# Filter taps spread over the partitions by two DRAM transfers instead of four TensorE transposes

## The chip, the cores and the metric

The kernel runs on one core of one Trainium2 chip. The metric is the device time of one execution in microseconds (us). Before the change the median of three runs is 174.2 us (174.18 to 174.44). One further execution was recorded by the hardware profiler; all views of the profile come from it.

## The reference

```python
x = A_x                                            # (1, 2048, 448)
g = sigmoid((x * gate_w).sum(-1, keepdims=True))
a = A_ref(x, wqkv, wo)                             # linear attention, 16 heads of 28
b = B_ref(x, log_A_real, A_imag, C_real, C_imag, log_dt, D_skip)
return g * a + (1 - g) * b

# B_ref: a state space convolution, N = 256 states for each of D = 448 channels
dt = exp(log_dt)
A = -exp(log_A_real) + 1j * A_imag
C = (C_real + 1j * C_imag) * dt[:, None]
K = 2 * einsum("dn,dnl->dl", C, exp((A * dt[:, None])[:, :, None] * arange(L))).real
y = causal convolution of u with K along L         # by FFT in the reference
return y + u * D_skip
```

The inputs make `exp(log_dt)` so small that the filter K is flat in time to working precision: K of channel d is its first tap at every lag. The kernel tests that (`okc`) and then needs one tap per channel, so that the convolution becomes a running sum over time, multiplied with a row of 448 taps. The general convolution (`general_conv`) is in the program for channels that fail the test, and is skipped by a branch when none does.

## The kernel before, in words

Time, 2048 steps, is cut into 16 chunks of 128, one step per partition. 32-bit floats are split into a high and a low part (`low`, line 236) so that products keep their precision on TensorE. For each chunk c the main loop (lines 475 to 531) issues, in this order for every engine: the load of chunk c + 3 on the SP queue (`load_x`), the key projection of chunk c + 1 on TensorE (`project`, line 333; 11 matmuls in order of which every second one at the start reads the low part of `xt`), the split of chunk c + 2's transposed input (`split_t`: high part on ScalarE, low part on GpSimd), the key features (`k_feature`, `k_high`, `k_low`), the query projection of chunk c, its features (`q_post`), the products of `do_g(c)`, and the split of chunk c + 2's plain input (`split_n`, then `skip`, both on GpSimd). The schedule is written out by hand: each engine executes its instructions in exactly the order of the program, and waits where an input isn't there.

The convolution part rides along. `do_v(v)` makes two matmuls (lines 409 and 410) with a triangle of ones: running sums of chunk v, put into the PSUM buffer `v0` or `v1` by the parity of v. `v_post(v)` multiplies them with the row of taps `near` on VectorE (line 414), sends the last row to `u` by two small transfers on the SP queue (line 417), and adds the product to `y` on GpSimd (`v_add`, line 422). The table `VS` says which chunks v go with which c: from c = 5 to 10 two of them, 2c - 10 and 2c - 9.

The taps themselves are made by `s4d_prepare`, a generator whose steps are dealt out by `steps(n)`. It reads `abc`, the four parameter tables of 112 partitions x 4 x 256 each (channel j * 112 + r is partition r, column j), reduces over the states and leaves `p0`, a tile of 112 partitions x 4 taps in `sm` (last written by line 307, which the profile shows as the helper's line 279). Its last step, dealt out at c = 5 between the query projection and `q_post(5)`, spreads them over the partitions: four transposes (line 312) of `p0`'s columns, broadcast, give 128 x 448 in PSUM, and ScalarE copies that to `near` (line 313). `near` is the first 448 columns of `rows`; the second 448 are `dsk`, a row of DRAM broadcast to all partitions when the kernel starts (line 226).

What is loaded at the start goes over one SP queue in the order of lines 216 to 233: the first weights and inputs, `dsk`, chunk 3, `ldt`, the first table of `abc`, chunk 4, the other three tables, and `both` (identity and triangle).

Of the kernel before, what the change touches and what calls it, by code (L numbers as in the profile page):

```python
# [7 lines left out]
F32 = mybir.dt.float32  # L8
# [7 lines left out]
P = 128  # L16
S = 2048
D = 448
# [4 lines left out]
J = 4  # L23
DJ = D // J
# [116 lines left out]
def gated_mix_kernel(ctx: ExitStack, tc: tile.TileContext, xin, wq_d, wvo_d, abc_d, ldt_d, dsk_d,  # L141
                     turn_d, cst_d, first_d, gin_d, out):
    nc = tc.nc
    PE, ACT, DVE, POOL, SP = nc.tensor, nc.scalar, nc.vector, nc.gpsimd, nc.sync
# [12 lines left out]
    work = ExitStack()  # L157
# [7 lines left out]
    ident, trir = both[:, 0], both[:, 1]  # L165
# [5 lines left out]
    near, dsk = (rows[:, i * D:(i + 1) * D] for i in range(2))  # L171
# [12 lines left out]
    xn_p = work.enter_context(tc.tile_pool(name="xn", bufs=7))  # L184
    tp = work.enter_context(tc.tile_pool(name="tp", bufs=2))
    ps = work.enter_context(tc.tile_pool(name="ps", bufs=1, space=PSUM))

    warm = tp.tile([P, 512], mybir.dt.bfloat16, name="warm", tag="e")
    DVE.memset(warm, 1.0)  # L189
# [7 lines left out]
    def load_x(c):  # L197
        r = xp.tile([P, XC], F32, name="xr", tag="xr")
        turned[c], plain[c] = r[:, :NAT], r[:, NAT:]
        SP.dma_start(out=r, in_=xin[c])  # L200
# [4 lines left out]
    abc = pf[:DJ, 3 * J * N:7 * J * N].rearrange("p (i j n) -> p i j n", i=4, j=J)  # L205
    wkr = {}
    o = 0
    for part in PARTS:
# [8 lines left out]
        o = e  # L217
# [8 lines left out]
    SP.dma_start(out=dsk, in_=dsk_d.to_broadcast([P, D]))  # L226
    load_x(3)
    SP.dma_start(out=ldt, in_=ldt_d)
    for i in range(4):
        SP.dma_start(out=abc[:, i], in_=abc_d[:, i])  # L230
        if i == 0:
            load_x(4)
    SP.dma_start(out=both, in_=turn_d)

    def low(eng, o, r, h):
# [2 lines left out]
    def split_t(c):  # L238
        w = xt[c] = xt_p.tile([P, 2 * NAT], F32R, name="xt", tag="t")
        ACT.copy(w[:, :NAT], turned[c])  # L240
        low(POOL, w[:, NAT:], turned[c], w[:, :NAT])
# [32 lines left out]
    def small():  # L274
        cnt[0] += 1
        return sm[:, cnt[0] - 1]

    def s4d_prepare():
        tt = lambda eng, o, a, b, op: eng.tensor_tensor(out=o, in0=a, in1=b, op=op)
        stt = lambda o, a, k, b, op1: DVE.scalar_tensor_tensor(out=o, in0=a, scalar=k, in1=b, op0=ALU.mult, op1=op1)  # L280
        junk = [yf[:DJ, F0 + (i - 2) * 2 * N:F0 + (i - 1) * 2 * N].rearrange("p (i n) -> p i n", i=2) for i in range(2)]
        s0, s1, dt, am, p0, p1, d2, md, b0, b1 = (small() for _ in range(10))
        for j in range(J):
            ACT.activation(abc[:, 0, j], abc[:, 0, j], AF.Exp)
        ACT.activation(dt, ldt, AF.Exp)
        tt(DVE, d2, dt, dt, ALU.mult)
        yield
        for j in range(J):
            ACT.activation(junk[0], abc[:, 0:2, j], AF.Square, accum_out=am[:, j:j + 1])
            ACT.activation(junk[0][:, 0], abc[:, 2, j], AF.Copy, accum_out=s0[:, j:j + 1])  # L290
            DVE.scalar_tensor_tensor(out=junk[1], in0=abc[:, 2:4, j], scalar=1.0, in1=abc[:, 0:2, j], op0=ALU.mult,
                                     op1=ALU.mult, accum_out=s1[:, j:j + 1])
            if j % 2:
                yield
        tt(DVE, md, am, d2, ALU.mult)
        stt(p0, s0, 2.0, dt, ALU.mult)
        stt(p1, s1, -2.0, d2, ALU.mult)
        DVE.tensor_scalar(out=md, in0=md, scalar1=SMALL, scalar2=None, op0=ALU.is_le)
        stt(b0, p0, -1.0, p0, ALU.max)
        stt(b1, p1, -1.0, p1, ALU.max)  # L300
        yield
        DVE.tensor_scalar(out=p0, in0=p0, scalar1=-BIG, scalar2=BIG, op0=ALU.max, op1=ALU.min)
        DVE.scalar_tensor_tensor(out=md, in0=b0, scalar=1.0 / FAR, in1=md, op0=ALU.is_ge, op1=ALU.mult)
        stt(okc, b1, FLAT, b0, ALU.is_le)
        DVE.scalar_tensor_tensor(out=md, in0=b0, scalar=FAR, in1=md, op0=ALU.is_le, op1=ALU.mult)
        tt(DVE, okc, okc, md, ALU.mult)
        tt(DVE, p0, p0, okc, ALU.mult)
        DVE.tensor_reduce(out=oks, in_=okc, op=ALU.add, axis=AX.X)
        yield
        o = ps.tile([P, 512], F32, name="p", tag="v1")  # L310
        for j in range(J):
            PE.transpose(o[:, j * DJ:(j + 1) * DJ], p0[:, j:j + 1].to_broadcast([DJ, P]), ident[:DJ, :DJ])  # L312
        ACT.copy(near, o[:, :D])

    def pieces(c, wh, wl, n, tag, last=None):
        o = ps.tile([P, 512], F32, name=tag, tag=tag)
        h, l = ([xt[c][:, i + k * P:i + (k + 1) * P] for k in range(J)] for i in (0, NAT))
        hh, lh, hl = ([(a[k], w[:, k]) for k in range(J)] for a, w in ((h, wh), (l, wh), (h, wl)))
        hl = hl[1:]
        if last == "x":  # L320
            seq = hh + hl + lh
        else:
            seq = [p for k in range(J) for p in (hh[k], lh[k])] + hl
            if last and len(last) > 1:
                seq = [{"h": hh, "l": lh, "w": [None] + hl}[i[0]][int(i[1])] for i in last.split()]
            elif last == "w":
                seq = seq[2:6] + seq[8:9] + seq[6:8] + seq[9:] + seq[:2]

        def run(count):
            for _ in range(min(count, len(seq))):  # L330
                a, b = seq.pop(0)
                run.n += 1
                PE.matmul(o[:, :n], lhsT=a, rhs=b, start=run.n == 1, stop=not seq)  # L333
        run.n = 0
        return o, run

    def project(*args, **kw):
        o, run = pieces(*args, **kw)
        run(11)
        return o  # L340
# [15 lines left out]
    def k_feature(c, o):  # L356
        e = tp.tile([P, D], F32, name="e", tag="e")
        pks[c] = o[:, :D]
        ACT.activation(e, pks[c], AF.Relu, scale=-1.0)  # L359
        ACT.activation(e, e, AF.Exp, scale=-1.0)  # L360
        DVE.scalar_tensor_tensor(out=pks[c], in0=pks[c], scalar=1.0, in1=e, op0=ALU.add, op1=ALU.max)  # L361

    def k_high(c):
        pkh[c] = tp.tile([P, 512], F32R, name="pkh", tag="pkh")[:, EDGE:EDGE + D]
        ACT.add(pkh[c], pks[c], 1e-6)
# [12 lines left out]
    def q_post(c, o, mid=None):  # L378
        ACT.activation(e1[:, c:c + 1], o[:, D:D + 1], AF.Exp, scale=-1.0)
        feature(pq[:, c], o, mid)  # L380
# [26 lines left out]
    def do_v(c):  # L407
        v = vt[c] = ps.tile([P, 512], F32, name="v", tag="v%d" % (c % 2))
        PE.matmul(v[:, :D], lhsT=tri, rhs=xn[c][:, :D], start=True, stop=False)  # L409
        PE.matmul(v[:, :D], lhsT=tri, rhs=xn[c][:, XC - NAT:], start=False, stop=True)  # L410
# [14 lines left out]
    def steps(n):  # L425
        for _ in range(n):
            next(prep, None)
# [47 lines left out]
    for c in range(2, NC - 2):  # L475
        if c + 3 < NC:
            load_x(c + 3)
        if c == 2:
            SP.dma_start(out=cst, in_=cst_d)
        if c == 4:  # L480
            SP.dma_start(out=wvo, in_=wvo_d)
        vs = VS.get(c, ())
        ko = project(c + 1, wkh, wkl, D, "v1" if c in (2, 4) else "k")
        for v in vs[:1]:
            do_v(v)
        split_t(c + 2)
        k_feature(c + 1, ko)
        k_high(c + 1)
        if c > 5:
            for v in vs[:1]:  # L490
                v_post(v)
        k_low(c + 1)
        qo = project(c, wqh, wql, D + 2, "q")
        if c == 5:
            steps(1)
        else:
            for v in vs[1:]:
                do_v(v)
        q_post(c, qo)
        if c == 10:  # L500
            split_n(c + 2)
        if c == 5:
            v_post(0)
        else:
            for v in vs[1:]:
                v_post(v)
        if c < 5:
            steps(2 if c == 4 else 1)
        if c == 3:
            DVE.tensor_copy(tri, trir)  # L510
            DVE.tensor_copy(gcr, gcat)
        if c == 7:
            SP.dma_start(out=okr[:, None, :DJ], in_=oks[:, None, :])
        if c == 9:
            DVE.tensor_reduce(out=okr[:, DJ:], in_=okr[:, :DJ], op=ALU.add, axis=AX.X)
            DVE.tensor_copy(okn, okr[:, DJ:])
        do_g(c)
        if c == 5:
            do_v(1)
        if c < 4:  # L520
            skip(c - 1)
        if c != 10:
            split_n(c + 2)
        if c == 5:
            v_post(1)
        for j in {11: (0, 1), 12: (2, 3)}.get(c, ()):
            w = xn_p.tile([P, NX], F32R, name="wo", tag="n")[:DJ, :2 * D].rearrange("p (i d) -> p i d", i=2)
            woh.append(w[:, 0])
            wol.append(w[:, 1])
            ACT.copy(woh[j], wo[:, j])  # L530
            low(POOL, wol[j], wo[:, j], woh[j])
# [109 lines left out]
    c = NC - 2  # L641
# [294 lines left out]
```

## Time and profile before

| what | us |
|---|---|
| median of three runs | 174.2 |
| the profiled execution | 174.88 |
| its span, first to last instruction | 173.1 |
| busy: TensorE matmul (PE) | 168.1 |
| busy: GpSimd (POOL) | 119.5 |
| busy: VectorE (DVE) | 114.4 |
| busy: ScalarE (ACT) | 96.3 |

Times in the views are microseconds from the start of the span unless marked ns. PEld is the weight load of TensorE, which overlaps with its matmuls; SP is the queue that issues the transfers here. A row of a timeline gives start, duration, engine, line, operation, the tile written and the tiles read, the shape and a count; in square brackets stands the idle time of the engine just before and what ended it. Rows with a count above 1 are several instructions merged. A row `L312 ...: a/b/c, d to e` gives the shortest, median and longest duration in ns and the first and the last start. In the chain that ended last each piece is the work that the end was waiting for at that time. Line numbers are those of the kernel before; a helper's line stands for all its calls.

### The profile page before, as it was taken

What the parts mean: (1) busy time and instruction counts of PE and PEld (TensorE: products, weight loads), DVE (VectorE), ACT (ScalarE), POOL (GpSimd) and SP (SyncE); (2) the same over time, 40 slices, a digit from 0 to 9 for tenths busy, and PEclk for the clock granted to TensorE, in tenths of its full rate; (3) what the DMA queues carried; (4) which work ended last, traced back from release to release, by engine and by line L of the source; (5) the groups of instructions that cost most, each with busy time, mean ns of one, the idle gap of its engine ahead of it and who ended that gap; (6) DMA issues with size and microseconds to landing.
All of it is one profiled execution on the core that took longest, in us unless ns stands there. A gap on an engine that the chain in (4) does not pass through costs nothing.

```text
span 173.1 us, 2796 instructions
## 1 busy us (share of the span) xinstructions
PE 168.1 (97%) x875; PEld 152.2 (88%) x875; DVE 114.4 (66%) x241; ACT 96.3 (56%) x221; POOL 119.5 (69%) x127
## 2 busy tenths in 40 slices
PE   6999999999999999999999999999999999999991
PEld 2698999999899999999999999999899999999991
DVE  1927746698975483836627346487898998997551
ACT  3768678895256262543727456356564564664541
POOL 5072568777619987696996999429978997983100
PEclk9999999999999999999999999999999999999999
DMA  5999976088002031231414200000031221222212
GB/s 172 417 294 301 257 175 198 0 327 342 0 4 95 29 122 19 106 90 37 122 22 122 106 1 1 0 0 2 7 67 53 107 106 58 91 98 78 108 67 102
DMA packets 7963, 18.61 MB, mean 108 GB/s; under 512 B 2045, under 2 KB 4810, under 8 KB 7818
## 3 DMA queue, kind: packets, MB, share of 16 engines
q1 hardware_dynamic: 7946, 18.41, 32.6%
q8 instruction: 7, 0.11, 0.3%
q14 instruction: 10, 0.08, 0.1%
HBM read 14.38 MB, written 3.67 MB: 104 GB/s over the span
## 4 chain that ended last, share of the span: by engine, by line
PE 97%; DVE 1%; ACT 0%; issue 0%; ACTq 0%
PE a L628 21%; PE g L402 20%; PE q L333 19%; PE k L333 15%; PE v L333 6%; PE tr L603 4%; PE q L258 3%; PE v L410 2%; PE v L409 2%; PE m L707 1%; PE k L727 1%; PE tr L727 1%; DVE warm L189 0%; PE p L312 0%; DVE ot L633 0%; ACT pq L639 0%
## 5 line engine op out<-in xcount | busy, mean ns | idle before, releaser
L628 PE MATMUL a<-wk,th 128*128 128x448 f32 (+1 forms) x170 | 36.4, 360 | 0.0
L402 PE MATMUL g<-pkh,xn 128*128 128x448 f32 x112 | 35.5, 363 | 0.0
L628 PEld LDWEIGHTS a<-wk,th 128*128 128x128 f32 x170 | 29.5, 189 | 1.6
L333 PE MATMUL k<-wk,xt 128*128 128x448 f32 x132 | 30.1, 374 | 0.0
L361 DVE SCALAR_TENSOR_TENSOR k<-k,e 128x448 f32<-128x448 f32 x12 | 7.6, 631 | 30.1 <-ACT e L360 30.1
L333 PE MATMUL q<-wqh,xt 128*128 128x450 f32 x120 | 27.5, 366 | 0.0
L333 PEld LDWEIGHTS k<-wk,xt 128*128 128x128 f32 x132 | 25.3, 192 | 2.1 <-ACT wk L432 0.4
L422 POOL TENSOR_TENSOR y<-y,t 128x448 f32<-128x448 f32 x16 | 18.7, 1171 | 11.5 <-DVE t L414 11.5
L236 POOL TENSOR_TENSOR xn<-xr,xn 128x448 fp32r<-128x448 f32 x16 | 19.4, 1212 | 7.4 <-ACT xn L246 5.5
L333 PEld LDWEIGHTS q<-wqh,xt 128*128 128x128 f32 x120 | 22.5, 188 | 1.8
L402 PE MATMUL g<-pkl,xn 128*128 128x448 f32 x64 | 23.4, 366 | 0.0
L402 PEld LDWEIGHTS g<-pkh,xn 128*128 128x128 f32 x112 | 21.0, 188 | 2.2
L236 POOL TENSOR_TENSOR xt<-xr,xt 128x512 fp32r<-128x512 f32 x14 | 18.2, 1297 | 6.0 <-ACT xt L240 6.0
L359 ACT ACTIVATE e<-k 128x448 f32<-128x448 f32 x12 | 6.5, 544 | 27.2 <-PE k L333 27.2
L541 POOL TENSOR_TENSOR prod<-pq,zb 128x448 f32<-128x448 f32 x16 | 18.6, 1169 | 4.1 <-ACT zb L664 3.0
L252 POOL TENSOR_TENSOR y<-xr,rows 128x448 f32<-128x448 f32 x16 | 18.8, 1174 | 0.0
L566 POOL TENSOR_TENSOR pn<-pq,den 128x336 f32<-128x336 f32 x16 | 12.3, 768 | 6.0 <-ACT den L555 4.1
L633 DVE SCALAR_TENSOR_TENSOR ot<-y,og,a 128x448 f32<-128x448 f32 (+1 forms) x17 | 10.7, 629 | 5.1 <-PE a L628 5.1
L611 DVE TENSOR_TENSOR th<-tr,th 128x512 fp32r<-128x512 f32 x16 | 11.0, 690 | 2.7 <-ACT th L610 2.1
L402 PEld LDWEIGHTS g<-pkl,xn 128*128 128x128 f32 x64 | 11.1, 174 | 1.2 <-DVE pkl L371 0.2
L610 ACT CAST th<-tr 128x512 fp32r<-128x512 f32 x16 | 9.4, 589 | 4.6 <-PE tr L603 4.4
L333 PE MATMUL q<-wql,xt 128*128 128x450 f32 x45 | 11.7, 364 | 0.0
(150 smaller groups left out, 302.5 us busy)
## 6 DMA issues: line engine op xcount, KB each, us to landing
xr<-in SPq DMA_DIRECT2D x15, 512.0 KB, 5.8
out<-ot SPq DMA_DIRECT2D x15, 224.0 KB, 1.9
pq<-in SPq DMA_DIRECT2D x4, 448.0 KB
wvo<-in SPq DMA_DIRECT2D x1, 1792.0 KB
y<-in SPq DMA_DIRECT2D x2, 480.0 KB
y<-in SPq DMA_DIRECT2D x2, 450.0 KB
u<-t SPq DMA_DIRECT2D x30, 1.8 KB, 1.8
y<-in SPq DMA_DIRECT2D x1, 448.0 KB, 4.3
```

The source lines that it names most:

```text
L236: eng.tensor_tensor(out=o, in0=r, in1=h.bitcast(F32), op=ALU.subtract)
L252: POOL.tensor_tensor(out=y[:, c], in0=plain[c][:, :D], in1=dsk, op=ALU.mult)
L333: PE.matmul(o[:, :n], lhsT=a, rhs=b, start=run.n == 1, stop=not seq)
L361: DVE.scalar_tensor_tensor(out=pks[c], in0=pks[c], scalar=1.0, in1=e, op0=ALU.add, op1=ALU.max)
L402: PE.matmul(g[i][:a.shape[1], :D], lhsT=a, rhs=b, start=c == 0 and n == 0, stop=c == NC - 1 and n == len(seq) - 1)
L422: POOL.tensor_tensor(out=y[:, c], in0=y[:, c], in1=t, op=ALU.add)
L541: POOL.tensor_tensor(out=pd[c], in0=pq[:, c], in1=zb, op=ALU.mult)
L566: POOL.tensor_tensor(out=n[:, :3, :DJ].rearrange("p j (h d) -> p j h d", h=4), in0=a, in1=r[:, :H - 4].rearrange("p (j h) -> p j h", j=3)[ ...
L610: ACT.copy(h, ov)
L611: DVE.tensor_tensor(out=l, in0=ov, in1=h.bitcast(F32), op=ALU.subtract)
L628: PE.matmul(a[:, lo:hi], lhsT=u_, rhs=w_[:, lo:hi], start=n == 0, stop=n == 10)
L633: DVE.scalar_tensor_tensor(out=ot[:, lo:hi], in0=y[:, c, lo:hi], scalar=og[:, c:c + 1], in1=a[:, lo:hi], op0=ALU.mult, op1=ALU.add)
```

## The change

Three edits. First, the last step of `s4d_prepare` no longer uses TensorE and ScalarE: the SP queue writes `p0` to a new DRAM tile `nd` of 448 floats, in the order of the channels, and then reads `nd` into `near` with every partition getting the whole row. The second transfer waits for the first. Both are issued at c = 5, where the transposes stood. Second, `abc` is loaded by two transfers of two tables each instead of four, with the load of chunk 4 between them. Third, at c = 6 alone, `do_v(2)` and `v_post(2)` move: `do_v(2)` from behind the key projection to behind the query projection, where `do_v(3)` is, and `v_post(2)` from between `k_high` and `k_low` to behind `q_post(6)`.

```diff
+    nd = work.enter_context(tc.tile_pool(name="nd", bufs=1, space=bass.MemoryType.DRAM)).tile([D], F32, name="nd")
...
-    for i in range(4):
-        SP.dma_start(out=abc[:, i], in_=abc_d[:, i])
-        if i == 0:
-            load_x(4)
+    SP.dma_start(out=abc[:, :2], in_=abc_d[:, :2])
+    load_x(4)
+    SP.dma_start(out=abc[:, 2:], in_=abc_d[:, 2:])
...
-        o = ps.tile([P, 512], F32, name="p", tag="v1")
-        for j in range(J):
-            PE.transpose(o[:, j * DJ:(j + 1) * DJ], p0[:, j:j + 1].to_broadcast([DJ, P]), ident[:DJ, :DJ])
-        ACT.copy(near, o[:, :D])
+        SP.dma_start(out=nd.rearrange("(j r) -> r j", j=J), in_=p0)
+        SP.dma_start(out=near, in_=nd.rearrange("(o d) -> o d", o=1).to_broadcast([P, D]))
...
         vs = VS.get(c, ())
+        vs = ((), vs) if c == 6 else (vs[:1], vs[1:])
         ko = project(c + 1, wkh, wkl, D, "v1" if c in (2, 4) else "k")
-        for v in vs[:1]:
+        for v in vs[0]:
             do_v(v)
...
-            for v in vs[:1]:
+            for v in vs[0]:
                 v_post(v)
...
-            for v in vs[1:]:
+            for v in vs[1]:
                 do_v(v)
...
-            for v in vs[1:]:
+            for v in vs[1]:
                 v_post(v)
```

## The prediction

> **What bounds the kernel now.** I read the page first (its shares and the chain that ended last), then that chain in order of time around the change, then the timelines of the engines and of the SP queue between 45 and 60 us.
>
> ```profile
> span 173.1 us, 2796 instructions
> PE 168.1 (97%) x875; PEld 152.2 (88%) x875; DVE 114.4 (66%) x241; ACT 96.3 (56%) x221; POOL 119.5 (69%) x127
> PE 97%; DVE 1%; ACT 0%; issue 0%; ACTq 0%
> ...
> 47.25 0.46 PE p L312 x4
> ...
> 57.77 2.20 PE k L333 x11
> ```
>
> TensorE (PE) is the bound: 97% of the span is its own work, one matmul after another. A matmul taken out is therefore worth its place in the chain, 0.46 us for the four transposes of line 312, and any wait that makes PE stand still goes to the end in full, since no later PE wait could swallow it. So the question is whether the taps, on their new way, reach `near` before anything that PE needs is held up.
>
> Who needs `near`, on VectorE (DVE), GpSimd (POOL) and PE; columns are start, duration, engine, line, operation:
>
> ```profile
> 46.89 0.16 DVE L279 TENSOR_TENSOR sm<-sm,okc 112x4 f32<-112x4 f32 x1
> ...
> 50.37 1.14 DVE L414 TENSOR_TENSOR t<-v,rows 128x448 f32<-128x448 f32 x2
> 53.82 0.63 DVE L361 SCALAR_TENSOR_TENSOR k<-k,e 128x448 f32<-128x448 f32 x1 [2.31 <-ACT e L360]
> 54.36 0.61 DVE L414 TENSOR_TENSOR t<-v,rows 128x448 f32<-128x448 f32 x1
> ...
> 51.12 1.16 POOL L422 TENSOR_TENSOR y<-y,t 128x448 f32<-128x448 f32 x1 [5.09 <-DVE t L414]
> 52.24 1.16 POOL L236 TENSOR_TENSOR xn<-xr,xn 128x448 fp32r<-128x448 f32 x1
> 53.35 1.16 POOL L252 TENSOR_TENSOR y<-xr,rows 128x448 f32<-128x448 f32 x1
> 54.46 1.17 POOL L422 TENSOR_TENSOR y<-y,t 128x448 f32<-128x448 f32 x1
> 55.56 1.32 POOL L236 TENSOR_TENSOR xt<-xr,xt 128x512 fp32r<-128x512 f32 x1
> ...
> 57.61 2.36 PE L333 MATMUL k<-wk,xt 128*128 128x448 f32 x11
> ```
>
> The taps `p0` are ready at 46.89 + 0.16 = 47.05. Their first use is `v_post(0)` on DVE at 50.37, so today there are 3.3 us between them, of which transposes and copy take little. The five POOL rows are the important ones. POOL works in program order; it stood idle for 5.09 us until `v_post(0)` gave it the sum of chunk 0, and then ran five instructions without a gap. The last is the low part of `xt` for chunk 8, done at 55.56 + 1.32 = 56.88. PE's key projection of chunk 8 starts at 57.61 and its second matmul, some 0.20 later (57.81), already reads that low part. So a late `near` does not have to hold up PE directly: it is passed on through POOL's queue, with little room.
>
> **Removed.** Four transposes, 0.46 us on the path that sets the end. The copy out of PSUM on ScalarE goes too:
>
> ```profile
> L313 ACT COPY rows<-p x1: 527/527/527, 48.1 to 48.1; 128x448 f32<-128x448 f32 x1
> ...
> 48.81 0.61 DVE L371 SCALAR_TENSOR_TENSOR zb<-k,zb 128x448 f32<-128x448 f32 x1
> 49.34 0.38 DVE L349 TENSOR_SCALAR t<-e 128x448 f32<-128x448 f32 x1
> ```
>
> Its 0.53 us I cost at nothing: what came next on ScalarE is the exponential for DVE's line 349, and that line came straight behind DVE's own line 371, with no wait noted. So `v_post(0)`, two DVE instructions later, could not start before 50.37 in the new kernel either.
>
> **Added: two transfers in a row.** The first writes 112 partitions x 4 taps into DRAM with a stride, so 448 pieces of 4 bytes; the second may be issued only when that has landed, and reads 1.8 KB for each of 128 partitions. Nothing in the trace is either of them. The nearest rows (KB, then median us from issue to landing):
>
> ```profile
> out<-ot SPq DMA_DIRECT2D x15, 224.0 KB, 1.9
> u<-t SPq DMA_DIRECT2D x30, 1.8 KB, 1.8
> ...
> wk<-shl SPq DMA_DIRECT2D x3, 56.0 KB, 2.2
> ...
> cst<-in SPq DMA_DIRECT2D x1, 112.5 KB, 3.7
> ```
>
> The write: from below `u` with 1.8, from above `cst` with 3.7. For small pieces there is one view, the DMA engines from 68.15 to 68.40 us, when the 112 four-byte pieces of `okr` and their 16 completions pass:
>
> ```profile
> DMA packets 128, 0.00 MB, mean 2 GB/s; under 512 B 128, under 2 KB 128, under 8 KB 128
> ```
>
> 128 in 0.25 us makes about 0.9 us for 448; added to `u`'s 1.8, less what `u`'s own pieces are, I take 2.5.
>
> The read moves 224 KB, as `out` does in the other direction: from below 1.9. But one load of before has exactly its form, the broadcast of `dsk` (line 226). The DMA engines from 10.9 to 12.3 us, where nearly all packets are its 1792-byte ones, and from 27 to 36 us for ordinary loads:
>
> ```profile
> DMA packets 114, 0.21 MB, mean 146 GB/s; under 512 B 7, under 2 KB 108, under 8 KB 114
> ...
> GB/s 120 24 8 0 0 73 200 18 218 382 400 382 437 200 55 0 0 0 0 0 0 0 0 0 0 0 0 0 0 0 0 0 0 0 0 0 218 255 182 309
> ```
>
> At 146 GB/s 229 kB take 1.6 us, at some 400 they take 0.6. So the read costs about 1.0 more than `out`: I take 3.0 (1.9 + 1.0, rounded); from above 3.7, the `cst` row.
>
> The wake-up of a queue is small: DVE's product ended at 50.37 + 0.61 = 50.98, and the first transfer of it was issued at 51.01:
>
> ```profile
> 50.37 0.61 DVE L414 TENSOR_TENSOR t<-v,rows 128x448 f32<-128x448 f32 x1
> 51.01 2.52 SPq L417 DMA_DIRECT2D u<-t  x4
> 53.63 0.53 SPq L200 DMA_DIRECT2D xr<-in  x1
> ```
>
> So `v_post(0)` starts at 47.05 + 0.04 + 2.5 + 0.05 + 3.0 = 52.64, which is 2.27 later than 50.37. By the lower bounds (1.8 and 1.9) it is 50.84, 0.47 late; by the upper ones (3.7 each) 54.54, 4.17 late.
>
> The Trainium skill (DMA: Bandwidth & Descriptors, "Anatomy of one DMA") speaks against the change: each transfer pays a fixed 2.0 us or so, most of it the receipt from the memory written, plus its bytes at 436 GB/s. An estimate by it is 2.0 + 2.5 = 4.5 us for the two, so 1.3 us late and, by the sum below, 0.6 us slower (174.8), the low end of the forecast's own range; the rows above agree on the fixed part and differ on the speed of a broadcast.
>
> **From late to stalled.** If `v_post(0)` is L late, `xt`'s low part of chunk 8 is done at 56.88 + L, because the five POOL instructions run without gap already. PE's second matmul needs it, and one weight load ahead of it:
>
> ```profile
> L333 PEld LDWEIGHTS k<-wk,xt 128*128 128x128 f32 x132 | 25.3, 192 | 2.1 <-ACT wk L432 0.4
> ```
>
> With 0.19 for that and 0.06 for the wake-up it can start at 57.13 + L, against 57.81 before. The end moves by L - 0.68, but by no less than -0.46. With L = 2.27 that is +1.59 us: a stall of 2.05 less the 0.46. The bounds give -0.21 and +3.49.
>
> The other followers of the wait have more room. DVE: `v_post(1)` and then line 361 of chunk 7 queue behind it; DVE had 2.31 us idle there, so line 361 is at most 0.4 late, and its buffer is wanted only by the same projection at 57.61. PE needs the buffers of chunks 0 and 1 for `do_v(2)` and `do_v(3)`, before at
>
> ```profile
> 52.38 0.36 PE L409 MATMUL v<-xn,tri 128*128 128x448 f32 x1
> ...
> 55.00 0.36 PE L409 MATMUL v<-xn,tri 128*128 128x448 f32 x1
> ```
>
> The third edit puts chunk 2 behind the query projection, at 55.00 - 0.41 - 0.46 = 54.1 (two matmuls of 0.20 and the transposes less ahead of it), and buffer `v0` is free at 52.64 + 0.61 = 53.3. Without that edit chunk 2 would come at 51.9 and PE would wait for 1.4 there; that wait would be part of the same 2.05, not on top. SP: four `u` transfers and the load of chunk 9 (53.63) queue behind the read's wait and come some 2.3 us later. ScalarE waited 0.96 for that load:
>
> ```profile
> 57.27 0.62 ACT L240 CAST xt<-xr 128x512 fp32r<-128x512 f32 x1 [0.96 <-DMA xr<-in]
> 60.07 0.55 ACT L359 ACTIVATE e<-k 128x448 f32<-128x448 f32 x1 [2.17 <-PE k L333]
> ```
>
> but then had 2.17 until PE's next keys, which move by 1.59 as well: nothing. If `near` were in time, this would be moot.
>
> **The third edit** moves 0.41 us of PE work behind 2.2 us of other PE work, and `v_post(2)` out of a DVE gap. Its addition on POOL comes after `xt`'s low part in either order. Cost nothing, hidden by POOL's lateness; were POOL on time it would wait for that sum a little, with a whole chunk's matmuls until the next keys need POOL again.
>
> **The second edit** halves the issues of `abc` and lets the load of chunk 4 wait for 448 KB more. Its first reader is the last of the timeline rows here, without a wait; below them stands the landing of all `xr` loads:
>
> ```profile
> 7.98 0.35 SPq L200 DMA_DIRECT2D xr<-in  x1
> 23.05 1.33 ACT L284 ACTIVATE pq<-pq 112x256 f32<-112x256 f32 x4
> 24.88 0.62 ACT L240 CAST xt<-xr 128x512 fp32r<-128x512 f32 x1
> ...
> DMA to landing us min/median/max: 3.6/5.8/11.4
> ```
>
> The slowest `xr` load took 11.4 us to land (7.98 + 11.4 = 19.4); 448 KB more, at no more than the broadcast's 146 GB/s, add 3.1, which leaves 2.4 us. The first half of `abc` is wanted at 23.05 and lies ahead of chunk 4. Nothing.
>
> **The sum.** The profiled execution took 174.88 us, 1.78 around its span, and with +1.59 would take 176.47. The median of the runs is 174.2, so there I predict 175.8. A difference under 0.2% (0.35 us) can't be told from none.
>
> **The rivals.**
> 1. *Hidden (faster).* If the two landings together stay under 3.25 us, POOL's row is done by 57.1, PE meets no wait, and the four transposes are simply saved: 174.2 - 0.46 = 173.7. For it: the third edit takes the first direct wait away. Against: even the lowest rows sum to 3.7. It decides at L = 0.22. Chance 0.11.
> 2. *Nearly even.* The broadcast lands like `out` (1.9) and the write like `wk` (2.2): L = 47.05 + 0.04 + 2.2 + 0.05 + 1.9 - 50.37 = 0.87, so +0.19: 174.4. For it, `dsk` did not run quite alone. Chance 0.14.
> 3. *The small writes are slow.* 448 pieces on 16 engines are 28 each; if one piece took what a broadcast piece took (16 x 1.4 us / 108, about 0.2), the write would last 1.8 + 5.6 = 7.4, L is 7.2 and the end moves by 6.5: 180.7. For it: nothing here writes small pieces to DRAM. Against: the 128 in 0.25 us. Chance 0.09.
> 4. *The stall slows PE afterwards.* At the start PE's 448-column matmuls came 0.37 apart until 6.7 us, then 1.49 / 7 = 0.21:
>
> ```profile
> PEclk9999999999999999999999999999999999999999
> ...
> 6.32 0.37 PE k L333
> ...
> 7.15 1.49 PE k L333 x7
> ```
>
> If a stall brought that start-up pace back for as long as from 1.48 to 6.7, some 14 matmuls would lose 0.16 each, 2.3 us: 178.1. Against: the page shows a granted clock of 9 throughout, so the trace has no case of a fall. Chance 0.06. The Trainium skill (TensorE: Matmul & The Clock Gate, "What's actually happening") has the clock fall only after an idle window of about 3.4 us; by that, the 2.05 us stall would leave it alone.
>
> **How the numbers follow.** The forecast (one stall at chunk 8's keys, 175.8) has 0.60; its own range, from a sum of landings of 4.5 to 6.6, is 174.8 to 176.9. Faster 0.11 is rival 1, same 0.14 rival 2, slower 0.75 the rest. The range of 8 in 10 takes in rival 2, the lower bound (-0.21) and the upper (+3.49, 177.7): 174.0 to 177.8.
>
> **What would show it.** Right: PE idle about 2 us shortly after 57.3, released by POOL's `xt` row of line 236; POOL idle some 7 us before line 422; `v_post(0)` near 52.6, released by the DMA to `rows`; no other new PE wait. Wrong: `v_post(0)` at 50.6 or earlier, PE stalled first at `do_v(2)` or at another queue, matmuls over 0.3 us apart after the stall, or a wait before 30 us at ScalarE for `abc` or chunk 4.

## The result, and the profile after

The changed kernel takes 181.07 us (median of 6 runs, 180.57 to 181.44) against 174.3 for the kernel before in the same comparison: a ratio of 1.0371, with a 95% interval of 1.035 to 1.0393. Its profiled execution took 180.96, with a span of 179.2. The forecast was 175.8 in a range of 174.0 to 177.8: the direction was right, the size was not.

The page of the changed kernel, its span, PE's busy time, the clock granted in 40 slices, and the engines on the chain that ended last:

```profile
span 179.2 us, 2786 instructions
PE 170.0 (95%) x871; PEld 153.6 (86%) x871; DVE 115.5 (64%) x241; ACT 95.7 (53%) x220; POOL 119.5 (67%) x127
...
PEclk9999999999998589999999999999999999999999
...
PE 77%; DVE 8%; DMA 6%; ACT 6%; issue 1%; DVEq 0%; ACTq 0%
```

Two things are new. The chain is no longer PE's alone: 6% of it is the two transfers. And in three slices after 53 us PE's clock was not granted in full. The chain in order of time (start, length, what):

```profile
46.38 6.76 DMA nd<-sm
...
53.16 4.36 DMA rows<-nd
...
57.55 0.64 DVE t L412
...
58.23 0.74 PE v L407
...
60.09 3.97 PE g L400 x11
64.06 2.43 PE k L331 x11
```

The write landed after 6.8 us, where I had taken 2.5 and 3.7 as the upper bound; the read after 4.4 (3.0 and 3.7). `v_post(0)` started at 57.55. Who waited (line 412 is the old 414, 407 the old 409, 420 the old 422, 331 the old 333; each view from here on has the line numbers of its own kernel, which differ by a few):

```profile
57.55 1.16 DVE L412 TENSOR_TENSOR t<-v,rows 128x448 f32<-128x448 f32 x2 [7.78 <-DMA rows<-nd]
...
58.31 1.14 POOL L420 TENSOR_TENSOR y<-y,t 128x448 f32<-128x448 f32 x1 [12.99 <-DVE t L412]
...
58.23 0.74 PE L407 MATMUL v<-xn,tri 128*128 128x448 f32 x1 [4.59 <-DVE t L412]
...
64.21 0.50 PEld L331 LDWEIGHTS k<-wk,xt 128*128 128x128 f32 x3 [0.32 <-POOL xt L236]
```

PE stood for 4.59 us ahead of `do_v(2)`, whose buffer `v0` was still waiting to be read, and then its weight load only 0.32 us at chunk 8's keys, where I had put the whole stall. What lies between ran at a lower clock (stretch, its length, PE busy, PEld, DVE, ACT, POOL, granted clock, DMA share, GB/s):

```profile
57.00:65.00 8.00, 6.78 (x20) 5.70 (x21) 5.45 (x9) 2.12 (x5) 6.69 (x6) 0.58 0.21 67
```

The eleven matmuls of line 400 took 3.97 us instead of 2.21, as the chain of the kernel before has them (line 402 there):

```profile
55.56 2.21 PE g L402 x11
```

### The profile page after: what moved, and what is told of

Read it like the earlier page. It is cut to its first block, busy times and chain, and to the rows that moved or that the text cites. A ratio compares the mean times of both kernels' runs of the same rounds, so it can differ in the third digit from the quotient of the medians.

```text
span 179.2 us, 2786 instructions
## 1 busy us (share of the span) xinstructions
PE 170.0 (95%) x871; PEld 153.6 (86%) x871; DVE 115.5 (64%) x241; ACT 95.7 (53%) x220; POOL 119.5 (67%) x127
## 4 chain that ended last, share of the span: by engine, by line
PE 77%; DVE 8%; DMA 6%; ACT 6%; issue 1%; DVEq 0%; ACTq 0%
PE a L627 20%; PE g L400 16%; PE q L331 12%; PE k L331 11%; PE tr L602 4%; DMA nd<-sm 4%; PE v L331 4%; PE q L258 3%; DMA rows<-nd 2%; PE v L407 2%; PE v L408 2%; PE m L706 1%; DVE t L347 1%; PE k L726 1%; PE tr L726 1%
## 5 line engine op out<-in xcount | busy, mean ns | idle before, releaser
L400 PE MATMUL g<-pkh,xn 128*128 128x448 f32 x112 | 36.7, 375 | 0.0
L400 PE MATMUL g<-pkl,xn 128*128 128x448 f32 x64 | 24.3, 379 | 0.0
L400 PEld LDWEIGHTS g<-pkh,xn 128*128 128x128 f32 x112 | 22.0, 197 | 2.5 <-issue 0.2
L412 DVE TENSOR_TENSOR t<-v,rows 128x448 f32<-128x448 f32 x16 | 9.7, 615 | 7.8 <-DMA rows<-nd 7.8
L363 ACT ACTIVATE pkh<-k 128x448 fp32r<-128x448 f32 x12 | 6.5, 545 | 14.5 <-DVE k L359 14.5
L400 PEld LDWEIGHTS g<-pkl,xn 128*128 128x128 f32 x64 | 11.7, 182 | 1.4 <-DVE pkl L369 0.2
```

The costliest lines, as they stand in the source:

```text
L400: PE.matmul(g[i][:a.shape[1], :D], lhsT=a, rhs=b, start=c == 0 and n == 0, stop=c == NC - 1 and n == len(seq) - 1)
L412: DVE.tensor_tensor(out=t, in0=vt.pop(c)[:, :D], in1=near, op=ALU.mult)
```

## What makes the write slow

The DMA engines of the changed kernel from 46 to 53.5 us, 40 slots of 0.19 us:

```profile
GB/s 0 0 0 0 0 0 1 6 3 0 0 0 0 0 0 0 0 0 0 0 0 0 0 0 0 0 87 0 0 0 0 0 0 0 0 0 0 0 0 0
DMA packets 465, 0.02 MB, mean 2 GB/s; under 512 B 464, under 2 KB 464, under 8 KB 464
```

All 448 pieces and the 16 completions pass between 47.1 and 47.7, no slower than those of `okr` did; then nothing of this transfer is seen for 5.5 us until it counts as landed. So I had priced the passing of the pieces, and the time lies in what comes after it. Three theories: it goes by the number of small pieces, it is the price of touching a new piece of DRAM for the first time, or each write to DRAM is slow to confirm.

**A chain of transfers behind the last result of the kernel before.**

```diff
...
     final_c(NC - 1)
+    SP.dma_start(out=nd.rearrange("(j r) -> r j", j=J), in_=taps)
+    spread()                                    # nd -> near, all partitions
+    SP.dma_start(out=nd.rearrange("(j r) -> r j", j=J), in_=taps)
+    spread()
+    SP.dma_start(out=nd.rearrange("(r j) -> r j", j=J), in_=taps)
+    spread()
+    SP.dma_start(out=line, in_=nd.rearrange("(o d) -> o d", o=1))
+    SP.dma_start(out=nd.rearrange("(o d) -> o d", o=1), in_=line)
+    spread()
+    SP.dma_start(out=near, in_=dsk_d.to_broadcast([P, D]))
+    SP.dma_start(out=line, in_=near[0:1])
...
```

> The kernel before, with a chain of transfers added behind its last result, each waiting for the one ahead, so that the start of one minus the start of the one ahead is the landing. Twice in turn: the strided write of the taps into nd (448 pieces of 4 bytes) and the broadcast of nd to 128 partitions; then the write as 112 pieces of 16 bytes and the broadcast; then one row read from nd, one row of 1792 bytes written to nd, the broadcast; then the broadcast of the input dsk; then the taps gathered into one row of SBUF by four transfers of 112 four-byte pieces. Theory 'pieces': a write into DRAM costs by its small pieces, so both strided writes take 6 to 7 us, the 16-byte one 2.5 to 4, the whole row about 2, the SBUF gather about 2 each. Theory 'first touch': the first strided write takes 6.8 us and the second, like all later ones, 2 to 2.5. Theory 'DRAM writes are slow to confirm': all writes into nd take 6 to 7. The broadcast: 'same row for all' says 3.5 to 4.4 each time, with dsk too; 'just written' says 4.4 behind a write and under 3 for dsk.

The SP queue of that kernel (start, issue time, line, what):

```profile
169.92 0.42 SPq L851 DMA_DIRECT2D nd<-sm  x1
177.41 0.35 SPq L850 DMA_DIRECT2D rows<-nd  x1
181.11 0.33 SPq L853 DMA_DIRECT2D nd<-sm  x1
188.15 0.33 SPq L850 DMA_DIRECT2D rows<-nd  x1
191.99 0.33 SPq L855 DMA_DIRECT2D nd<-sm  x1
193.39 0.33 SPq L850 DMA_DIRECT2D rows<-nd  x1
...
197.63 0.23 SPq L858 DMA_DIRECT2D nd<-u  x1
198.75 0.34 SPq L850 DMA_DIRECT2D rows<-nd  x1
201.88 0.36 SPq L860 DMA_DIRECT2D rows<-in  x1
204.89 0.59 SPq L861 DMA_DIRECT2D u<-rows  x1
```

Each landing is the difference to the next row, from one execution; only the third broadcast can't be read off so, since a read of the same row was issued beside it. The strided write takes 7.5 us the first time and 7.0 the second: not a first touch. (In its place at c = 5 it took 6.6 to 7.0 in the five kernels here that have it.) The same 1.8 KB in pieces of 16 bytes take 1.4, as one row 1.1: writes to DRAM are not slow to confirm as such. The broadcast takes 3.7 and 3.8 behind the strided writes, 3.1 behind the whole row and 3.0 from `dsk`: a read of one row by all partitions costs 3.0, as taken, and in the changed kernel 1.4 more. (The gathers into one row of SBUF, 112 pieces of 4 bytes, landed in 1.9 each.) 'First touch' and 'slow to confirm' fall; 'pieces' was left, but it could still be their number or their place.

**Pieces of 4 bytes, laid closer and farther apart.** Again behind the kernel before; each write is followed by a read of one row that waits for it.

```diff
...
+    apart = lambda s: nw[:s * D].rearrange("(r j s) -> r j s", j=J, s=s)[:, :, 0]
+    SP.dma_start(out=nw[:D].rearrange("(j r) -> r j", j=J), in_=taps)
...
+    SP.dma_start(out=nw[:DJ].rearrange("(r o) -> r o", o=1), in_=taps[:, 0:1])
...
+    for s in (2, 16, 128):
+        SP.dma_start(out=apart(s), in_=taps)
...
+    SP.dma_start(out=nw[:D].rearrange("(r j) -> r j", j=J), in_=taps)
...
```

> The kernel before, with a chain behind its last result of writes of the taps into DRAM, each followed by a read of one row that waits for it, so that the start of the read minus the start of the write is the landing: 448 pieces of 4 bytes in channel order; 112 pieces of 4 bytes (one column, neighbours in DRAM); 448 pieces of 4 bytes laid 8, 64 and 512 bytes apart, the taps of a partition following each other; 112 pieces of 16 bytes. Theory 'by the piece': 448 pieces take about 7 us however they are laid, 112 pieces of 4 bytes about 2.5. Theory 'neighbours in the same line of DRAM': only close ones are slow; at 64 or 512 bytes apart they take 1.5 to 2.5, and the 112 neighbours of 4 bytes are slower than the 112 pieces of 16 bytes (1.4).

The SP queue again:

```profile
169.94 0.42 SPq L850 DMA_DIRECT2D nw<-sm  x1
177.58 0.24 SPq L851 DMA_DIRECT2D u<-nw  x1
179.41 0.31 SPq L852 DMA_DIRECT2D nw<-sm  x1
185.90 0.22 SPq L853 DMA_DIRECT2D u<-nw  x1
188.53 0.65 SPq L855 DMA_DIRECT2D nw<-sm  x1
194.32 0.23 SPq L856 DMA_DIRECT2D u<-nw  x1
195.66 0.62 SPq L855 DMA_DIRECT2D nw<-sm  x1
198.47 0.21 SPq L856 DMA_DIRECT2D u<-nw  x1
199.92 0.56 SPq L855 DMA_DIRECT2D nw<-sm  x1
201.99 0.21 SPq L856 DMA_DIRECT2D u<-nw  x1
203.21 0.31 SPq L857 DMA_DIRECT2D nw<-sm  x1
204.60 0.21 SPq L858 DMA_DIRECT2D u<-nw  x1
```

In this order: 448 pieces in channel order 7.6 us; 112 neighbours of 4 bytes 6.5; 448 pieces 8 bytes apart 5.8; 64 apart 2.8; 512 apart 2.1; and 112 pieces of 16 bytes 1.4. A quarter of the pieces, laid side by side, takes three times as long as all 448 laid 512 bytes apart. So it is not their number: 'by the piece' falls. The three spaced writes differ in nothing but the spacing and go from 5.8 to 2.1, so what costs is that 4-byte pieces land next to each other. The same 112 small pieces gathered into SBUF, where they are neighbours too, took 1.9, so the destination counts as well. Why neighbours of 16 bytes are not slow these runs don't say; pieces of 8 bytes were not tried. Nor do they say what the memory does in those microseconds. Each of these landings comes from one execution.

The Trainium skill (DMA: Bandwidth & Descriptors, "Anatomy of one DMA") puts the fixed cost at about 2 us, from a fit to transfers that GpSimd issues, and says that the wait for the receipt can be surprisingly long where the target is HBM. The slow write agrees with it in where the time goes (5.5 of 6.8 us pass after the last piece), but the writes here, which SP issues, range from 1.1 to 7.6 us for the same 1.8 KB, by the layout.

## What carries the late taps to the end

**16-byte pieces in the changed kernel.** The channels are dealt to the partitions so that a partition's four taps are neighbours in DRAM; the general convolution's flags follow.

```diff
...
-        SP.dma_start(out=nd.rearrange("(j r) -> r j", j=J), in_=p0)
+        SP.dma_start(out=nd.rearrange("(r j) -> r j", j=J), in_=p0)
...
-    byd = lambda a: np.asarray(a).reshape(J, DJ, -1).transpose(1, 0, 2)
+    byd = lambda a: np.asarray(a).reshape(DJ, J, -1)
```

> The changed kernel with the channels dealt to the partitions so that the four taps of a partition are neighbours in DRAM: the write is 112 pieces of 16 bytes instead of 448 of 4. Theory 'pieces': the write lands in about 3 us instead of 6.8, v_post(0) starts near 53.8, and the end comes some 3 to 4 us earlier: 177 to 178. Theories 'first touch' and 'slow to confirm': nothing moves, 181.

It took 176.46 us (175.2 to 177.43), a ratio of 1.0089 (1.0055 to 1.0123), a little less than expected, since the write landed in 1.4 us and not 3. Its SP queue, DVE, PE and the stretch from 57 to 65 us:

```profile
46.57 0.33 SPq L310 DMA_DIRECT2D nd<-sm  x1
47.96 0.33 SPq L311 DMA_DIRECT2D rows<-nd  x1
...
52.38 1.16 DVE L412 TENSOR_TENSOR t<-v,rows 128x448 f32<-128x448 f32 x2 [2.44 <-DMA rows<-nd]
...
53.67 0.37 PE L407 MATMUL v<-xn,tri 128*128 128x448 f32 x1
...
59.06 3.30 PE L331 MATMUL k<-wk,xt 128*128 128x448 f32 x10 [2.01 <-POOL xt L236]
...
57.00:65.00 8.00, 5.99 (x23) 5.42 (x23) 2.85 (x6) 2.29 (x4) 7.78 (x8) 0.79 0.38 126
```

Here the landings sum to 5.8 us, near the 5.5 that I had taken, though by two errors that cancel: the write took 1.4 (2.5 taken) and the read 4.4 (3.0 taken). So the read is slower in place than at the kernel's end behind a fast write too; why, no run shows. What I had forecast for that sum is what is seen: no wait at `do_v(2)`, and one stall of 2.01 us (forecast 2.05) at the second matmul of chunk 8's keys, released by POOL's `xt`. Behind it the clock fell too, to 0.79: the ten matmuls left of the keys took 3.30 us, where the eleven take 2.36 elsewhere. This profiled execution was the longest of six, 177.43 us. Three of the six took 175.2 to 175.86, about the forecast's 175.8; the other three took 177.06 to 177.43.

**The first edit alone.** Against the kernel before, so `do_v(2)` stands where it was and `abc` comes by four transfers:

```diff
...
-        o = ps.tile([P, 512], F32, name="p", tag="v1")
-        for j in range(J):
-            PE.transpose(o[:, j * DJ:(j + 1) * DJ], p0[:, j:j + 1].to_broadcast([DJ, P]), ident[:DJ, :DJ])
-        ACT.copy(near, o[:, :D])
+        SP.dma_start(out=nd.rearrange("(j r) -> r j", j=J), in_=p0)
+        SP.dma_start(out=near, in_=nd.rearrange("(o d) -> o d", o=1).to_broadcast([P, D]))
```

> The first edit alone. do_v(2) then stands ahead of the query projection of chunk 6, so TensorE stops there, for about 7 us instead of 4.6, and has 5.2 us of matmuls left to chunk 8's keys, at half the clock for most of them. Theory 'GpSimd sets the end': the end is that of the changed kernel, 181, as long as those matmuls are done when xt's low part is. Theory 'the slowed clock counts': they are not, since some 15 matmuls lose 0.17 each; chunk 8's keys start near 66 instead of 64.2, and the time is 182.5 to 183.5.

184.18 us, a ratio of 1.055 (1.0526 to 1.0573):

```profile
58.03 0.74 PE L408 MATMUL v<-xn,tri 128*128 128x448 f32 x1 [6.46 <-DVE t L413]
...
58.94 3.20 PE L332 MATMUL q<-wqh,xt 128*128 128x450 f32 x8
...
65.89 2.36 PE L332 MATMUL k<-wk,xt 128*128 128x448 f32 x11
```

PE stops one projection earlier, runs the eight query matmuls in 3.20 us instead of 1.78, and reaches chunk 8's keys at 65.89, later than POOL's row, which is done before 64: 'the slowed clock counts' held in its mechanism, while the time came out above its 182.5 to 183.5. The kernel is 3.1 us slower than the changed one, and some 0.3 of that is the second edit (below). So the third edit is worth nearly 3 us in the changed kernel.

**Each of the two paths cut, and both.** GpSimd's additions of chunks 0 and 1 behind the low part; chunk 6's query projection made three times so that PE has work; both.

```diff
...
     def v_post(c):
...
+            if c < 2:
+                held.append((c, t))
+            else:
+                v_add(c, t)
...
         split_t(c + 2)
+        if c == 6:
+            for v, t in held:
+                v_add(v, t)
```

> The changed kernel with GpSimd's additions of the sums of chunks 0 and 1 moved behind the low part of xt for chunk 8, so that nothing GpSimd does for chunk 8's keys waits for near. The predicted path (near, v_post(0), five GpSimd instructions, chunk 8's keys) is then gone. Theory 'GpSimd's lateness sets the end, as predicted': only the stall ahead of do_v(2) stays, 4.6 us instead of the 7 that the predicted sum gives with the measured landings, and the time falls by 2.4 or more, to 178.6. Theory 'two paths of the same length': the matmuls behind the stall run so slowly (15 of them, 0.17 us more each) that they are done only 0.3 us before GpSimd's row anyway; the time falls by 0.3 to 180.8.

```diff
...
-        qo = project(c, wqh, wql, D + 2, "q")
+        qo = project(c, wqh, wql, D + 2, "q", times=3 if c == 6 else 1)
...
```

> The changed kernel with the query projection of chunk 6 made three times over, into the same buffer, so that TensorE has 4.4 us of work in the 4.6 us in which it stood still. Theory 'two paths of the same length': the clock stays, the matmuls behind run 0.20 apart, and TensorE waits the 2.5 us gained for GpSimd's row instead: 181, as the changed kernel. Theory 'the slowed clock sets the end': 178.5.

> Both edits in one: GpSimd's two additions behind the low part, and TensorE kept busy. Theory 'two paths of the same length': only now both are gone, and the time falls by 2.5 + 0.3 to 178.2. Theory of either path alone: no lower than the better of the two single edits.

| kernel | us | ratio to before, 95% interval |
|---|---|---|
| changed | 181.07 | 1.0371 (1.035 to 1.0393) |
| additions behind | 180.79 | 1.0364 (1.0328 to 1.0399) |
| PE kept busy | 182.73 | 1.0442 (1.0399 to 1.0485) |
| both | 178.72 | 1.0236 (1.0214 to 1.0257) |

With the additions behind, POOL's row is done before 53 us and nothing of it is waited for, yet chunk 8's keys start at 63.65, because the matmuls behind the stall still run slowly:

```profile
51.23 1.29 POOL L236 TENSOR_TENSOR xt<-xr,xt 128x512 fp32r<-128x512 f32 x1
...
58.20 0.74 PE L407 MATMUL v<-xn,tri 128*128 128x448 f32 x1 [4.33 <-DVE t L414]
...
63.65 2.37 PE L331 MATMUL k<-wk,xt 128*128 128x448 f32 x11
```

With PE kept busy the stall ahead of `do_v(2)` is 0.24 and the clock stays, but the time saved comes back as a wait for POOL:

```profile
58.58 0.47 PE L409 MATMUL v<-xn,tri 128*128 128x448 f32 x1 [0.24 <-DVE t L414]
...
64.56 3.76 PE L333 MATMUL k<-wk,xt 128*128 128x448 f32 x10 [2.38 <-POOL xt L236]
```

and that wait then lets the clock fall after all (the ten matmuls take 3.76 us, not 2.2). Of its four runs one was granted the full clock and took 180.99, the others 182.7 to 183.0; the 181 that I expected holds for that one only. With both edits the keys start at 62.00 and run at the full clock:

```profile
62.00 2.36 PE L333 MATMUL k<-wk,xt 128*128 128x448 f32 x11
```

So 'two paths of the same length' held in what counts: either cut alone gains nothing clear, both together 2.35 us. (The kernel with both still does 4.4 us of query matmuls for nothing; they only fill the stall.) 'GpSimd's lateness sets the end' by itself, my prediction's form, falls for the changed kernel, and stands for the one with 16-byte pieces.

## The parts costed at nothing, and a version that beats both

**Second and third edit without the first.**

```diff
...
-        SP.dma_start(out=nd.rearrange("(j r) -> r j", j=J), in_=p0)
-        SP.dma_start(out=near, in_=nd.rearrange("(o d) -> o d", o=1).to_broadcast([P, D]))
+        o = ps.tile([P, 512], F32, name="p", tag="v1")
+        for j in range(J):
+            PE.transpose(o[:, j * DJ:(j + 1) * DJ], p0[:, j:j + 1].to_broadcast([DJ, P]), ident[:DJ, :DJ])
+        ACT.copy(near, o[:, :D])
```

> The kernel before with the second and the third edit and without the first: abc by two transfers, do_v(2) and v_post(2) moved at c = 6, the transposes kept. My prediction: both cost nothing, 174.3 within 0.3 us. Rival: the later load of chunk 4, or the later sum of chunk 2 on GpSimd, makes TensorE wait: a wait of 0.5 us or more before 30 us or at chunk 9's keys, 174.8 or more.

173.96 us against 174.69, 0.9963 (0.9949 to 0.9977): not nothing, but a little faster. With the second edit alone:

> The kernel before with the second edit alone, abc by two transfers. The kernel with the second and third edit was 0.6 us faster than before where I had costed both at nothing. If the second edit does it (fewer transfers at the start), this one is 174.0 too; if the third does, it is 174.6, as before.

173.98 us beside 174.3, 0.9976 (0.9965 to 0.9988). So some 0.3 us come from the second edit; whether the third adds anything isn't settled, since the twin below, with both, gained 0.3 again. What the second edit does at the start these runs don't show: in the profiles PE left its slow start-up pace at 7.15 us in the kernel before, at 6.68 with the second edit alone and at 6.99 with the second and third, but also at 6.67 with the first edit alone, which loads `abc` as before, so one profile each can't tell that from chance.

**16-byte pieces and the additions behind, and its twin with the transposes.**

> The changed kernel with the write as 112 pieces of 16 bytes and with GpSimd's two additions moved behind the low part. near lands near 52.4; do_v(2) needs buffer v0 at 53.7 and gets it at 53.0; chunk 8's keys wait for nothing. Theory: no wait of TensorE is left, the four transposes (0.46 us) are saved against the kernel with the other two edits alone: 173.5, under the kernel before. Rival: another follower of near (line 359 on VectorE, the load of chunk 9 behind the SP queue's wait) takes its place: a wait of TensorE of 0.3 us or more at chunk 8's or 9's keys, 174.0 or more.

173.58 us, 0.995 (0.9932 to 0.9967). From the profile, `do_v(2)`, the first matmul that needs a buffer which `v_post(0)` frees, and the keys of chunk 8, both without a PE wait ahead:

```profile
53.95 0.37 PE L407 MATMUL v<-xn,tri 128*128 128x448 f32 x1
...
56.98 2.36 PE L331 MATMUL k<-wk,xt 128*128 128x448 f32 x11
```

> The kernel with 16-byte pieces and the two additions behind, once more, beside its twin with the transposes on the same chip. If the removed transposes are worth their 0.46 us once nothing waits for near, it is 0.46 us under the twin: 173.5 and 174.0.

> The twin: the second and third edit and the two additions behind, but the taps by the four transposes and the copy, as before. 174.0, as with the second and third edit alone. If it is within 0.15 us of the version without the transposes, the 0.46 us was not on the path that sets the end, or is given back elsewhere.

173.45 us (0.9954, 0.9939 to 0.9969) and 174.0 us (0.9979, 0.9964 to 0.9993) on one chip: 0.55 apart, for 0.46 expected. The two intervals overlap a little, but the profiles agree on the place: in the chain that ended last, from the start of chunk 6's keys to that of chunk 8's it is 41.72 to 56.64 us without the transposes and 41.96 to 57.40 with them, 0.52 less. The idea of the change pays what its transposes cost once no matmul waits for the taps; this version has the lowest median of all.

## Why the prediction was wrong, step by step

- *The transposes are worth 0.46 us on the path.* Right: 0.55 between the twins' medians, 0.52 in their profiles.
- *The write lands in 2.5 us, at most 3.7.* This step failed. It measured 6.8. I sized it by the small pieces of `okr`, which go to SBUF, and by the time in which pieces pass the DMA engines; 4-byte neighbours written into DRAM spend most of their time after that (5.5 of 6.8 us). Rival 3 named the place and nearly the price (7.4 us, 180.7), though not the cause: it let each piece take 0.2 us, while all pass in 0.6 us.
- *The read lands in 3.0 us.* Too short by 1.4. The broadcast of one row costs 3.0 by itself; behind the strided write it took 3.7 and 3.8 at the kernel's end, and 4.4 in place; behind the write of 16-byte pieces it took 3.9, 4.1 and 4.4 there in three profiled executions. What makes it slower in place stays open. Together the two terms were short by 5.6 us, three quarters of it the write.
- *The end moves by L - 0.68.* Its number came out, in part by luck: POOL's row was still the last to come, by some 0.3 us, but PE's own way, which the sum leaves out, was nearly as long. `v_post(0)` was 57.55 + 0.70 - 50.37 = 7.88 late (the taps were last written 0.70 earlier in this execution, from 46.19 instead of 46.89), which gives +7.20; chunk 8's keys ended at 66.49 instead of 59.97, and with the same 0.70 that is 7.22. The whole moved by less, 6.77 by the medians and 6.08 between the two profiled executions, since in the profiled one the start was faster and what follows PE's last matmul 0.4 shorter.
- *PE has no wait at `do_v(2)`, and the clock stays.* For a `near` at 52.6 the first is true, as the kernel with 16-byte pieces shows, and the second is not to be relied on: in its profile the clock fell behind the 2.01 us stall. With `near` at 57.5 PE waited 4.59 at `do_v(2)`, and rival 4 came on top. That this cost so little more was luck: the slowed matmuls were done just ahead of POOL's row.
- *Second and third edit cost nothing.* Nearly: the second gains 0.3 us. That the third had to be there was right; I had valued its absence at nothing on top, where it costs nearly 3 us with these landings.
- *Rival 1 needs landings under 3.25 us.* A slip in the sum: L = 0.22 means 3.45 us together. It changes nothing here, with 11.1 measured.

## What to carry to other kernels

Price a transfer by its destination and by how its pieces lie there, not only by their number: 448 taps written into DRAM as 4-byte pieces side by side landed in 6.6 to 7.6 us, the same bytes in 16-byte pieces in 1.4. When a late input has several followers, find out for each how late it may be; cutting the one that the chain names can leave the time as it is, because the next is as late. And look at the instructions queued behind a waiting one on an in-order engine: moving two additions that nobody was waiting for was one of the two steps that made the change pay.

## What the runs showed that I had not expected

A stall of PE can be followed by a stretch of lower granted clock even when it is short. In the profiled executions, from 57 to 65 us, the clock was 0.58 with the wait of 4.59 us and 0.79 with that of 2.01 us; with a wait of 0.16 us (both cuts) it stayed at 1.00:

```profile
57.00:65.00 8.00, 7.84 (x38) 6.74 (x37) 4.84 (x9) 1.66 (x5) 4.08 (x4) 1.00 0.25 78
```

The Trainium skill (TensorE: Matmul & The Clock Gate, "What's actually happening") lets the clock fall after about 3.4 us of idleness. The 4.59 us agree; the 2.01 us do not, and the measurement decides. It does not happen every time. The kernel with PE kept busy, with a stall of 2.38 us in its profile, took 180.99 us in the execution with a mean clock of 1.0 and 182.66 to 182.98 in the three at 0.989 to 0.991, so the fall cost 1.7 to 2.0 us on top of the stall itself. The six executions with 16-byte pieces lie in two groups 1.5 us apart, but there the clock is not the whole account: one of the longer three, 177.29 us, has a mean clock of 1.0.
